# Narrower warm-up matmuls and another waiting point for early loads, in a fused attention and gated-MLP kernel

## The chip, the cores and the metric

The kernel runs on one core of a Trainium2 chip. The time is device microseconds for one launch. Matrix products run on TensorE (PE in the profile, its weight loads PEld), elementwise work on VectorE (DVE), ScalarE (ACT) and GpSimd (POOL). SyncE (SP) computes nothing; its queue, and ScalarE's and GpSimd's, issue the loads and stores.

## What is computed

With S = 2048 tokens of width D = 512, in bf16:

```python
x = A_x; xn = layernorm(x)
# A: attention of 32 heads of 16, each token sees 8 keys, 2 tokens apart
q, k, v = split(xn @ A_wqkv)
logits = einsum(q, k[pos - 2*w]) * Dh**-0.5          # w = 0..7, masked where pos - 2*w < 0
a = einsum(softmax(logits), v[pos - 2*w]) @ A_wo
# B: gated MLP that mixes over tokens
z = gelu(xn @ B_w_in)                                # 512 -> 1792
z1, z2 = z[..., :896], layernorm(z[..., 896:])
g = einsum('ts,sf->tf', B_w_sp, z2) + B_b_sp[:, None]
b = (z1 * g) @ B_w_out
return x + a + b
```

## The kernel before

The tokens lie in 16 blocks of 128, and the blocks in four groups of four. For each block, VectorE takes the statistics (`bnst`, line 612, and `bnag`, 615), GpSimd the power -0.5 (`rstd`, 617) and VectorE normalises (`norm`, 626). Blocks 0 to 3 are transposed on TensorE (`xTr`, 642) and copied out of PSUM by ScalarE (`xTe`, 648); later blocks go through transposing transfers on SP's queue (`xTd`, 630). Block 0 takes a short way: it is only centred (`ctr`, 621), in two halves, goes through TensorE so, and its scale is applied with the GELU; its normalised form follows later (`xNr`, 661, copied out at 665).

Then TensorE computes, in this order: the second half of z for blocks 0 to 3 (`z2`, 818, two matmul groups of 448 columns a block, GELU on ScalarE at 829), q and k of the first group (694, copied out at 702), v of blocks 0 to 7 (676), and so on group by group; then z1 (841), the token mixing g (951) and the output products (1017 and 1021).

Every operation is a task with the keys that it reads and writes. A planner (`Plan.schedule`) gives each engine its order, for the parts that matter from lists written out by hand (`plan.orders`), and `emit` places semaphore waits from the keys. A key that is read also protects it: whoever writes the same key later waits for all its readers. Engines and queues work in order.

The early loads, in the order of the queues:

- SP: x blocks 0 and 1; the first half (rows 0 to 255) of two 448-column pieces of `w_in` that make z2 (`w_in2a` and `w_in2b`); x blocks 3, 4, 5; q and k weights; x blocks 6 and 7; v weights; then x blocks 8 and on, whose eight buffers are those of blocks 0 and on (`ld_x`, line 545, slot `b % 8`), between the transposes of blocks 4 to 7.
- ScalarE: a priming activation (590), which loads the GELU table and reads a constant that GpSimd sets (524); then the second half (rows 256 to 511) of both z2 pieces (555), told to wait for VectorE's first memset, `zeros`; then x block 2.

The loads of q, k (567) and x blocks 4 to 7 are told to wait until x block 1 has landed, by naming it as read. That also makes them readers of block 1's buffer, which x block 9 uses next.

TensorE begins with a warm-up that has no use but to keep it busy: eight matmuls of 512 columns on a constant of ones (584). A shorter filler of 320 columns follows the transposes of block 0. Each matmul has a weight load of its own, of 128 columns.

Of the kernel before, what the change touches and what calls it, by code (L numbers as in the profile page):

```python
# [14 lines left out]
class Plan:  # L15
# [297 lines left out]
DEFAULT_CFG = dict(  # L313
    xdma=4,
    fill=1,
    warm=8,
    fill0=1,
    perm=0,
)
# [2 lines left out]
def build_kernel(nc, A_x, A_wqkv, A_wo, B_x, B_w_in, B_w_sp, B_b_sp, B_w_out, out, report=False, sched_kw=None,  # L322
                 cfg=None, emit=True):
    cfg = dict(DEFAULT_CFG, **(cfg or {}))
# [77 lines left out]
    with ExitStack() as es:  # L402
# [10 lines left out]
        def A(name, n, o2_=0):  # L413
            return ar[:, off[name] + o2_: off[name] + o2_ + n]

        def AC(o_, dims):
            return bass.AP(tensor=ar, offset=o_, ap=[[AR, 128]] + [list(d) for d in dims])
# [92 lines left out]
        def dma(eng, fn, nbytes, chan, reads=(), writes=(), name="", xbar=False, prio=None, lat=1700.0):  # L510
            return T(eng, fn, reads=tuple(reads), writes=tuple(writes), name=name, prio=prio,
                     dma=dict(chan=chan, nbytes=nbytes, xbar=xbar, lat=lat))

        ident = A("ident", 128)
        zeros = A("zeros", 512)
# [5 lines left out]
          name="steps0")  # L521
        T("dve", lambda v: v.memset(FCa(foff["st6"] + 8, [[9, NB], [1, 1]]), LN_EPS * D), writes=["st_eps"], est=160,
          name="steps1")
# [4 lines left out]
          writes=["ident"], est=350, name="ident1")  # L528
# [3 lines left out]
          writes=[("KTpad", c, 0) for c in range(4)], est=200, name="ktpad", prio=2)  # L532
# [7 lines left out]
        def xin_ap(sl):  # L540
            return A("xin", 512, 512 * sl) if sl < 4 else A("xin2", 512, 512 * (sl - 4))

        def ld_x(b, eng="sp", after=()):
            sl = b % 8
            dma(eng, lambda e: e.dma_start(xin_ap(sl), x2[128 * b:128 * b + 128, :]), 128 * 512 * 2,
                ("xin", sl), reads=after, writes=[("xin", sl)], name="ldx%d" % b)
# [6 lines left out]
        def ld_win_h(nm, lo, n):  # L553
            for h in range(2):
                dma(("sp", "act")[h], (lambda h: lambda e: e.dma_start(  # L555
                    AC(off["w_in"] + lo + 2 * 1792 * h, [[1792, 2], [1, n]]),
                    B_w_in[256 * h: 256 * h + 256, lo: lo + n].rearrange("(c p) n -> p c n", p=128)))(h),
                    256 * n * 2, (nm, h), reads=["zeros"] if h else [], writes=[(nm, h)], name="ld%s_%d" % (nm, h))

        ld_x(0)  # L560
        ld_x(1)
        ld_win_h("w_in2a", FH, HF)
        ld_win_h("w_in2b", FH + HF, HF)
        ld_x(2, "act")
        ld_x(3, "sp")
        for which, eng in ((0, "sp"), (1, "sp")):
            dma(eng, (lambda which: lambda e: e.dma_start(
                AC(off["wqk"] + 512 * which, [[1024, 4], [1, 512]]),
                A_wqkv[:, 512 * which: 512 * which + 512].rearrange("(c p) n -> p c n", p=128)))(which),
                512 * 512 * 2, ("wqk", which), reads=[("xin", 1)],  # L570
                writes=[(("wq", "wk")[which], c) for c in range(4)],
                name="ld%s" % ("qk"[which]))
        for b in range(4, min(8, NB)):
            ld_x(b, "sp", after=[("xin", 1)])
        dma("sp", lambda e: e.dma_start(A("wv_raw", 2048).rearrange("p (c n) -> p c n", c=4),
                                        A_wqkv[:, 1024:1536].rearrange("(c p) n -> p c n", p=128)),
            512 * 512 * 2, "wv", writes=["wv_raw"], name="ldwv")
# [2 lines left out]
        def filler(n, name, est, prio=None, reads=(), w=512):  # L580
            def warm(t):
                last = None
                for i in range(n):
                    last = t.matmul(ps[:, 3584: 3584 + w], ones[:, :128], ones[:, :w], start=True, stop=True)
                return last
            T("pe", warm, reads=reads, writes=[("ps", 7)], est=est, name=name, prio=prio)

        filler(cfg["warm"], "warm", 400.0 * cfg["warm"])

        T("act", lambda a: a.activation(Fv("prime", 4), mhalf, ACTF.Gelu_apprx_tanh), reads=["mhalf"], writes=["prime"],  # L590
          est=-1200, name="actprime", tbl="gelu")
# [545 lines left out]
def bass_parallel_sum__sliding_local_dilated__mixer_gmlp__prompt_kernel(  # L1137
    nc, A_x, A_wqkv, A_wo, B_x, B_w_in, B_w_sp, B_b_sp, B_w_out, out
):
    build_kernel(nc, A_x, A_wqkv, A_wo, B_x, B_w_in, B_w_sp, B_b_sp, B_w_out, out)  # L1140
# [28 lines left out]
```

## Time and profile before

| | |
|---|---|
| time, median of 3 runs | 237.5 us (235.75 to 238.12) |
| the profiled execution's own time | 236.43 us |
| its span, from the first to the last instruction | 234.6 us |
| TensorE busy | 230.8 us (98%) |
| VectorE busy | 202.4 us (86%) |
| ScalarE busy | 118.8 us (51%) |
| GpSimd busy | 51.1 us (22%) |
| moved by DMA | 41.76 MB, mean 178 GB/s |

The busy times are unions over one engine's instructions. A matmul's record reaches from its issue to the modelled end of its pass, so records overlap, and TensorE's busy share says that it always had something under way, not that it ran at its peak. In rows of the timeline the columns are the start in us from the span's start, the length, the engine, the line, the operation with its tiles, and how many were merged; in brackets stands how long the engine had been idle before it and what released it.

### The profile page before, as it was taken

Reading aid. Unit: us, or ns where it says so; the run is one execution under the profiler, and the core shown is the slowest. Engines: PE = TensorE matmul, PEld = TensorE weight load, DVE = VectorE, ACT = ScalarE, POOL = GpSimd, SP = SyncE. Lnnn points to the kernel's source line nnn. Section 1 sums busy time; section 2 is a strip of 40 time slices with the busy share of each in tenths; the row PEclk is TensorE's granted clock in tenths of the full one; section 3 lists DMA queues with packets and bytes.
Section 4 is the critical chain, followed back from the end, with each engine's and each line's share of the span. In section 5 each row is a group of like instructions: output and inputs, shape, how many; then the busy total and the mean of one; then the engine's idle time right before and its main releaser. Section 6 shows DMA issues by size and latency. Waiting matters only on the chain.

```text
span 234.6 us, 2976 instructions
## 1 busy us (share of the span) xinstructions
PE 230.8 (98%) x1107; PEld 110.5 (47%) x1107; DVE 202.4 (86%) x231; ACT 118.8 (51%) x235; POOL 51.1 (22%) x67
## 2 busy tenths in 40 slices
PE   8999999999999999999999999999999999999995
PEld 2554455454554444444444444444444444444444
DVE  4787979998989989997999994999999999999600
ACT  3798488988989978953021124232223413201442
POOL 4454973771690050001201000010000000000000
PEclk9999999999999999999999999999999999999999
DMA  6976770299909899691529999999545987802322
GB/s 210 357 188 145 176 163 0 92 191 322 375 33 179 198 245 264 119 237 41 155 64 220 287 228 225 297 231 307 157 134 157 203 237 187 227 0 46 92 63 70
DMA packets 87166, 41.76 MB, mean 178 GB/s; under 512 B 66272, under 2 KB 86000, under 8 KB 87152
## 3 DMA queue, kind: packets, MB, share of 16 engines
q1 hardware_dynamic: 71072, 23.24, 47.0%
q10 hardware_dynamic: 14640, 14.13, 20.1%
q0 software_dynamic: 1440, 4.21, 5.8%
q8 instruction: 9, 0.15, 0.3%
q14 instruction: 5, 0.04, 0.1%
HBM read 20.05 MB, written 5.26 MB: 108 GB/s over the span
## 4 chain that ended last, share of the span: by engine, by line
PE 95%; DMA 2%; DVE 1%; ACT 1%; POOL 0%; ACTq 0%; issue 0%
PE ps L951 41%; PE ps L694 12%; PE ps L1021 10%; PE ps L841 10%; PE ps L818 9%; PE ps L1017 6%; PE ps L676 6%; DMA arena<-in_A_x_dram 2%; ACT L590 0%; DVE fpool L612 0%; PE ps L642 0%; POOL fpool L617 0%; ACTq L555 0%; DVE arena L626 0%; ACT arena L1030 0%
## 5 line engine op out<-in xcount | busy, mean ns | idle before, releaser
L951 PE MATMUL ps<-arena 128*128 128x512 bf16 x448 | 97.5, 379 | 0.0
L951 PEld LDWEIGHTS ps<-arena 128*128 128x128 bf16 x448 | 43.8, 98 | 52.8
L945 ACT ACTIVATE ps<-arena 128x512 f32<-128x512 bf16 x28 | 16.5, 599 | 56.9 <-DVE arena L958 56.6
L718 DVE TENSOR_TENSOR arena<-arena 128x4096 bf16<-128x4096 bf16 x16 | 36.1, 2284 | 0.5 <-ACT arena L702 0.4
L976 DVE TENSOR_TENSOR arena<-arena 128x4096 bf16<-128x4096 bf16 x16 | 36.3, 2286 | 0.2
L980 DVE TENSOR_TENSOR arena<-arena 128x4096 bf16<-128x4096 bf16 (+1 forms) x16 | 28.1, 1755 | 0.3
L694 PE MATMUL ps<-arena 128*128 128x512 bf16 x128 | 28.3, 379 | 0.0
L723 DVE TENSOR_TENSOR arena<-arena 128x4096 bf16<-128x4096 bf16 x12 | 27.5, 2288 | 0.2
L1021 PE MATMUL ps<-arena 128*128 128x512 bf16 (+2 forms) x126 | 27.1, 355 | 0.0
L818 PE MATMUL ps<-arena 128*128 128x448 bf16 x128 | 26.2, 357 | 0.1
L841 PE MATMUL ps<-arena 128*128 128x512 bf16 x112 | 24.3, 379 | 0.0
L694 PEld LDWEIGHTS ps<-arena 128*128 128x128 bf16 x128 | 14.5, 113 | 13.2
L1030 ACT ACTIVATE arena<-ps 128x512 bf16<-128x512 f32 (+2 forms) x17 | 9.5, 559 | 21.4 <-PE ps L1021 20.5
L958 DVE TENSOR_TENSOR arena<-ps,arena 128x512 bf16<-128x512 f32 x28 | 19.1, 683 | 0.1
L1021 PEld LDWEIGHTS ps<-arena 128*128 128x128 bf16 x126 | 13.6, 113 | 11.0
L818 PEld LDWEIGHTS ps<-arena 128*128 128x128 bf16 x128 | 12.2, 98 | 11.7 <-issue 0.7
L846 ACT ACTIVATE arena<-ps 128x512 bf16<-128x512 f32 x28 | 15.9, 595 | 3.2 <-PE ps L841 2.7
L702 ACT ACTIVATE arena<-ps 128x1024 bf16<-128x1024 f32 x16 | 16.3, 1021 | 2.4 <-PE ps L694 1.6
L829 ACT ACTIVATE arena<-ps 128x448 bf16<-128x448 f32 x30 | 16.2, 546 | 2.2 <-issue 0.2
L841 PEld LDWEIGHTS ps<-arena 128*128 128x128 bf16 x112 | 11.0, 98 | 13.1
L708 POOL COPY arena<-arena 128x16 bf16<-128x16 bf16 x12 | 14.6, 1224 | 9.9 <-ACT arena L829 5.0
L1017 PE MATMUL ps<-arena 128*128 128x512 bf16 (+2 forms) x72 | 16.8, 355 | 0.0
(65 smaller groups left out, 193.5 us busy)
## 6 DMA issues: line engine op xcount, KB each, us to landing
arena<-vscr ACTq DMA_DIRECT2D x8, 1152.0 KB, 7.8
arena<-in_A_x_dram ACTq DMA_DIRECT2D x17, 128.0 KB, 5.0
vscr<-arena POOLq DMA_DIRECT2D x16, 128.0 KB, 2.5
arena<-in_A_x_dram SPq DMA_DIRECT2D x15, 128.0 KB, 3.9
out_dram<-arena ACTq DMA_DIRECT2D x15, 128.0 KB, 1.9
arena<-in_A_wqkv_dram SPq DMA_DIRECT2D x3, 512.0 KB, 6.2
ascr<-arena POOLq DMA_DIRECT2D x4, 256.0 KB, 4.0
arena<-ascr POOLq DMA_DIRECT2D x4, 256.0 KB, 3.3
```

Source lines behind the costliest of these rows:

```text
L694: last = t.matmul(bank(k + which), AC(off["wqk"] + 1024 * dc + col0, [[4, 128]]), AC(off["xnT"] + dc * S + 512 * j, [[1, 512]]), start=(dc ...
L718: T("dve", lambda v: v.tensor_tensor(pbv, qb, kb, ALU.mult), reads=[("QT", c, j), ("KT", c, j), ("KTpad", c, j)], writes=[("pb", s_)], est ...
L723: T("dve", lambda v: v.tensor_tensor(A("pb", 4096, 4096 * a), A("pb", 4096, 4096 * a), A("pb", 4096, 4096 * b), ALU.add), reads=[("pb", b) ...
L818: last = t.matmul(ps[:, 512 * k: 512 * k + HF], st, AC(off["w_in"] + 1792 * dc + c0, [[1, HF]]), start=(h == first and dc == 2 * h), stop= ...
L841: lastm = t.matmul(bank(k), AC(off["w_in"] + 1792 * dc + 128 * fc, [[1, 128]]), AC(off["xnT"] + dc * S + 512 * j, [[1, 512]]), start=(dc = ...
L945: T("act", lambda a: a.activation(bank(k), A("bbc", 512, 512 * tc), ACTF.Copy), reads=["bbc"], writes=[("ps", k)], est=c_act(512), name="g ...
L951: last = t.matmul(bank(k), AC(off["z2"] + FH * sh + 128 * fc, [[1, 128]]), AC(off["wT"] + WSL * r_ + sh * 512, [[1, 512]]), start=False, s ...
L958: T("dve", lambda v: v.tensor_tensor(uv, bank(k), uv, ALU.mult), reads=[("ps", k)], writes=[("z1T", fc, tc)], est=c_dve(512) + 20, name="u ...
L976: T("dve", (lambda iv, tv, av: lambda v: v.tensor_tensor(tv, iv, av, ALU.mult))(iv, tv, av), reads=[("attn", j), ("Ve", par)], writes=[("V ...
L980: T("dve", (lambda n: lambda v: v.tensor_tensor(AC(off["Vs"], [[4096, 2], [1, n]]), AC(off["Vs"], [[4096, 2], [1, n]]), AC(off["Vs"] + n, ...
L1017: t.matmul(po, AC(off["OT"] + 512 * ot_pos(tb) + 128 * cc, [[1, 128]]), AC(off["wo"] + 512 * cc + c0, [[1, n]]), start=False, stop=False, ...
L1021: last = t.matmul(po, AC(off["z1T"] + fc * S + t0, [[ts, 128]]), AC(off["w_out"] + 512 * fc + c0, [[1, n]]), start=False, stop=(fc == FC - ...
```

## The change

Three things change, and the hand-written orders stay as they are.

- The warm-up is 28 matmuls of 146 columns (4088 columns) where it was 8 of 512 (4096). The planner's estimate for it is nearly the same (3192 ns for 3200).
- The loads of q, k and x blocks 4 to 7 wait for the second half of `w_in2b`, which ScalarE's queue loads, where they waited for x block 1. They all stand on SP's queue behind x block 3.
- The second halves of the z2 weights on ScalarE's queue no longer wait for `zeros`.

As the wait no longer names x block 1, x block 9 no longer waits for the loads of q, k and blocks 4 to 7. In the order that the planner makes, it moves ahead of the four transposing transfers of blocks 4 to 7 on SP's queue. All other engines keep their order.

```diff
 DEFAULT_CFG = dict(
     xdma=4,
     fill=1,
-    warm=8,
+    warm=28,
...
-                    256 * n * 2, (nm, h), reads=["zeros"] if h else [], writes=[(nm, h)], name="ld%s_%d" % (nm, h))
+                    256 * n * 2, (nm, h), writes=[(nm, h)], name="ld%s_%d" % (nm, h))
...
-                512 * 512 * 2, ("wqk", which), reads=[("xin", 1)],
+                512 * 512 * 2, ("wqk", which), reads=[("w_in2b", 1)],
...
         for b in range(4, min(8, NB)):
-            ld_x(b, "sp", after=[("xin", 1)])
+            ld_x(b, "sp", after=[("w_in2b", 1)])
...
-        filler(cfg["warm"], "warm", 400.0 * cfg["warm"])
+        filler(cfg["warm"], "warm", 114.0 * cfg["warm"], w=146)
```

The filler that both use:

```python
def filler(n, name, est, prio=None, reads=(), w=512):
    def warm(t):
        for i in range(n):
            last = t.matmul(ps[:, 3584: 3584 + w], ones[:, :128], ones[:, :w], start=True, stop=True)
        return last
    T("pe", warm, reads=reads, writes=[("ps", 7)], est=est, name=name, prio=prio)
```

## The prediction

> **What bounds the kernel now.** I read the page's busy shares first, then the chain that ended last (in order of time: start, length, what), then who waited for whom on TensorE over the whole run.
>
> ```profile
> PE 230.8 (98%) x1107; PEld 110.5 (47%) x1107; DVE 202.4 (86%) x231; ACT 118.8 (51%) x235; POOL 51.1 (22%) x67
> ...
> 2.17 5.09 DMA arena<-in_A_x_dram
> ...
> 10.23 0.80 PE ps L818 x4
> 13.53 6.91 PE ps L694 x32
> 20.44 6.91 PE ps L676 x32
> ...
> PE ps L584 <- PEq L1154: 0.8, 1, 0.8
> PE ps L642 <- DVE arena L626: 0.3, 1, 0.3
> ```
>
> Only two waits stand for TensorE in the whole run, and the last ends at 9.35 us. From 10.23 us the chain is matmuls piece on piece to 232 us, so a change to the head is worth what it moves that stretch, and no more. Ahead of it the chain is one load: x block 2, issued third on ScalarE's queue (2.17 us), landed at 7.26, then its statistics, POOL's power and its normalisation. These are the rows of the head, from the timeline (start, length, what, idle before it and its releaser):
>
> ```profile
> 4.39 0.61 PE L642 MATMUL ps<-arena 128*128 128x128 bf16 x4
> ...
> 6.11 0.41 DVE L626 TENSOR_SCALAR arena<-arena,fpool 128x512 bf16<-128x512 bf16 x1 [0.46 <-POOL fpool L617]
> ...
> 6.98 0.39 PE L642 MATMUL ps<-arena 128*128 128x128 bf16 x4
> ...
> 7.29 0.69 DVE L612 BATCH_NORM_STATS2 fpool<-arena 128x6 f32<-128x512 bf16 x1 [0.77 <-DMA arena<-in_A_x_dram]
> ...
> 7.30 0.66 ACT L648 ACTIVATE arena<-ps 128x256 bf16<-128x256 f32 x2 [1.81 <-PE ps L642]
> ...
> 9.30 0.21 ACT L829 ACTIVATION_READ_ACCUMULATOR arena<-ps,fpool 128x1 f32 x1
> ...
> 9.34 0.23 PEld L642 LDWEIGHTS ps<-arena 128*128 128x128 bf16 x4 [0.74 <-DVE arena L626]
> ...
> 9.67 0.66 ACT L648 ACTIVATE arena<-ps 128x256 bf16<-128x256 f32 x2 [0.15 <-PE ps L642]
> ...
> 10.38 0.10 PEld L818 LDWEIGHTS ps<-arena 128*128 128x128 bf16 x1 [0.16 <-ACT arena L648]
> ```
>
> Three engines are close to one another here. VectorE waits 0.77 us for x block 2. TensorE's weight loads wait 0.74 us for that block's normalisation (9.34). But ScalarE, from 7.30 on, waits only 0.15 us (9.67) before block 2's evictions, and TensorE needs those at 10.38. That 0.15 us is what decides.
>
> **Part 1: x block 2 sooner.** These are ScalarE's second z2 load and x block 2 with their time from issue to landing, the DMA by stretch (the last number is GB/s), and two issues ahead of them:
>
> ```profile
> L555 ACTq DMA_DIRECT2D arena<-in_B_w_in_dram x1: 482/482/482, 1.7 to 1.7; - x1
> DMA to landing us min/median/max: 4.3/4.3/4.3
> L545 ACTq DMA_DIRECT2D arena<-in_A_x_dram x1: 488/488/488, 2.2 to 2.2; - x1
> DMA to landing us min/median/max: 5.1/5.1/5.1
> ...
> 1.50:3.00 1.50, 1.50 (x5) 0.59 (x4) 0.00 (x0) 0.72 (x2) 0.82 (x3) 1.00 0.68 131
> 3.00:7.26 4.26, 4.12 (x20) 1.45 (x18) 2.87 (x8) 0.66 (x2) 1.31 (x2) 1.00 1.08 367
> ...
> 0.73 0.10 POOL L524 MEMSET fpool<- 128x4 f32 x1 [0.29 <-POOLq L1154]
> 1.16 0.47 ACTq L555 DMA_DIRECT2D arena<-in_B_w_in_dram  x1
> ```
>
> 1.5 x 131 + 4.26 x 367 = 1760 KB had moved when x block 2 landed. The four x blocks and four z2 pieces that TensorE needs first are 1442 KB (by their shapes, 4 x 131 + 4 x 229); so some 300 KB of blocks 4, 5 and q went ahead of it. Held back, they free 300/367 = 0.8 us: landing near 6.45. Not holding ScalarE's z2 loads for the memset moves ScalarE's three issues from 1.16, 1.66 and 2.17 to at earliest about 0.9 (the prime activation still stands in front and waits for POOL's memset at 0.83): 0.2 to 0.3 us, on a DMA that moves only 131 GB/s up to 3.0. I take landing at 6.3 to 6.5. The bounds are 7.26 (the order on the wire is unchanged) and 6.2.
>
> Then the gain is cut down step by step. VectorE finishes block 1's normalisation at 6.52, so statistics of block 2 start at 6.55, not 7.29: 0.74 us. Block 2's transposes then are ready at about 8.6, but TensorE's earlier work ends at 9.34 - 0.74 = 8.60, or 0.1 later with the last matmul: 0.65 us remain. ScalarE, in order, is busy from 7.30 to 9.51 with work that hangs on block 1 and the z2 weights, so its eviction of block 2 starts at 9.52 in place of 9.67: **0.15 us** remain, and TensorE's 10.38 becomes 10.23. What could move ScalarE's 7.30 is block 1's transposes at 6.98; they stand in order behind z2 matmuls of block 0, which are not waiting for a load but run slowly:
>
> ```profile
> 6.05 0.15 PEld L818 LDWEIGHTS ps<-arena 128*128 128x128 bf16 x1
> 6.42 0.10 PEld L818 LDWEIGHTS ps<-arena 128*128 128x128 bf16 x1 [0.21 <-issue]
> 6.61 0.10 PEld L818 LDWEIGHTS ps<-arena 128*128 128x128 bf16 x1
> ```
>
> The pitch of 448-column matmuls is 0.37 us up to 6.42 and 0.19 us after it, though the clock column says 1.00 throughout. So the z2 weights' earlier landing (5.96, needed at 6.05) buys nothing. Term: -0.15 us, bounds 0 and -0.55 (the pitch falls one group sooner, block 1's transposes go at 6.6, right after the normalisation that ends at 6.52: 0.38 more).
>
> **Part 2: 28 narrow warm-ups.** 28 x 146 = 4088 columns for 4096. The wide ones go at one per 0.425 us:
>
> ```profile
> 2.00 0.15 PEld L584 LDWEIGHTS ps<-const-bfloat16-1.0 128*128 128x128 bf16 x1 [0.28 <-issue]
> 2.43 0.15 PEld L584 LDWEIGHTS ps<-const-bfloat16-1.0 128*128 128x128 bf16 x1 [0.28 <-issue]
> ...
> 4.69 0.31 PE L642 MATMUL ps<-arena 128*128 128x128 bf16 x1
> ```
>
> By columns, a narrow one takes 146/512 x 0.425 = 0.121 us, 28 of them 3.39 us against 3.40. What is added is 20 weight loads. The nearest row for a narrow matmul with a weight load of its own before the fast pitch is block 0's four transposes, at 4.39 to 4.69: three steps in 0.30 us, 0.10 each, half of that set by VectorE's second half. So a 0.12 us pitch hides the load: term 0. Bounds: nothing below (the columns are the same), and above as the rival on the other side.
>
> The Trainium skill ("TensorE: Matmul & The Clock Gate", Part 3, The mechanism) says that a weight load overlaps matmuls in flight only when its row group differs, and these fill all rows. By that rule the warm-up would take 28 x (0.12 + 0.15) = 7.5 us and the sum would be +2.9 us. The trace disagrees: four transposes, each with a load, fit into 0.61 us.
>
> **Part 3: the loads behind x block 3.** SP's queue waits at block 4 for ScalarE's second z2 load, in place of x block 1. Behind it stand blocks 4, 5, q, k, 6, 7, v, 8 and on. These are SP's issues of blocks 4 and 5, of q and k with their landing, and TensorE's first weight loads that follow q:
>
> ```profile
> L545 SPq DMA_DIRECT2D arena<-in_A_x_dram x2: 340/386/432, 3.8 to 4.2; - x2
> L567 SPq DMA_DIRECT2D arena<-in_A_wqkv_dram x2: 434/471/508, 4.6 to 5.1; - x2
> DMA to landing us min/median/max: 4.9/5.6/6.2
> ...
> 13.18 2.89 PEld L694 LDWEIGHTS ps<-arena 128*128 128x128 bf16 x14
> ```
>
> ScalarE's second z2 load landed at 1.66 + 4.3 = 5.96, and will a little earlier. So block 4 goes out at 5.5 to 6.0 in place of 3.8, q at 6.5 to 7.0 in place of 4.6, k half a us behind. The bytes ahead of k are the same; added is a pause on the wire from 6.4 (the first 1442 KB are through) to about 7.0 (I allow the new issue 1.3 us until its bytes move; the 131 GB/s up to 3.0 show such a start), 0.4 to 0.9 us. So k lands at 5.1 + 6.2 + 0.4 to 0.9 = 11.7 to 12.2, q at about 10.5 to 11. TensorE wants q at 13.18 and k 0.86 us later (32 matmuls take 6.91). Cost 0, hidden by z2 of blocks 2 and 3; if that cover goes, every us late costs a us. Upper bound, with both taking the longest time seen for a 512 KB piece, v's:
>
> ```profile
> L575 SPq DMA_DIRECT2D arena<-in_A_wqkv_dram x1: 434/434/434, 6.7 to 6.7; - x1
> DMA to landing us min/median/max: 6.9/6.9/6.9
> ...
> 20.36 0.69 DVE L612 BATCH_NORM_STATS2 fpool<-arena 128x6 f32<-128x512 bf16 x1 [1.58 <-DMA arena<-in_A_x_dram]
> ```
>
> q at 7.0 + 6.9 = 13.9 against 13.0: +0.9 us. v then lands near 15.9, wanted at 20.44. Blocks 6 and 7 land some 0.5 us late for VectorE, and TensorE wants their transposes only with V of these blocks, from 20.44 + 6 x 0.86 = 25.6 on: the cover is many times the delay.
>
> One load also moves: x block 9 reuses block 1's buffer. Before, the loads told to wait for block 1 counted as its readers, so block 9 stood behind four transposes; now it goes ahead of them. VectorE's 1.58 us wait at 20.36 should go. The chain has no VectorE there: 0 us, and the order of everything else is the same.
>
> **Sum.** -0.15 + 0 + 0 = -0.15 us against the profiled 236.43 us (span 234.6, 1.8 around it), which lies 1.1 us under the median 237.5. On the median's footing: 237.35, given as **237.3 us**. The runs shown spread by 2.4 us, so 1% is about what a measurement of this kernel can tell from no change; the forecast is "no difference".
>
> **The rivals.**
> - *Nothing moves at all*: the queues share the wire so that holding back blocks 4 and 5 doesn't bring block 2. For it: block 2 was issued ahead of blocks 4 and 5 (2.17 against 3.8) and may owe them nothing. Against it: the 300 KB. 237.5 us; 0.2.
> - *The warm-up is paced by its weight loads* (the other side). TensorE's warm-up ends at 4.18 and the first transposes wait for VectorE until 4.39, so it decides from a pitch of 3.62/28 = 0.129 us. If the 0.15 us loads set the pitch, 4.2 us: 0.5 us late; if nothing overlaps, 7.5 us, first transposes at 8.3, block 1's at about 9.9 in place of 6.98: +2.9, 240.4 us. Against it: the 0.10 us step. 0.07.
> - *q or k late*: +0.9 us, 238.3 us. For it: q is issued 2 us later and fewer than 2 us lie between landing and use. Against: the wire. 0.08.
> - *The fast pitch comes at another moment*: if not at 6.42 but a stretch as long as the warm-up (3.4 us) later, ten 448-column matmuls and six transposes cost 10 x 0.18 + 6 x 0.05 = 2.1 us more, less the 0.65 us idle: +1.5, 238.9 us; sooner: -0.55, 236.9 us. Nothing in the change asks for either. 0.05 each.
>
> **How the numbers follow.** Forecast 0.55, the rest as above. All but the unhidden weight loads stay within 1% of 237.5; I give that extreme 0.05, and two mishaps together or the runs' spread (the lowest shown is 0.7% under the median, the highest 0.3% over) 0.08: slower 0.13. Faster by over 1% would need 2.4 us out of a head whose TensorE waits are 0.8 + 0.3: only spread, 0.07. Same 0.80. The range goes from the lowest run shown less 0.35 (235.4) to the late clock with a little of the spread (239.4).
>
> **What would show it.** Right: SP's block 4 issued at 5.5 to 6.0; block 2's statistics at 6.55; the weight-load wait at 9.34 shrinks to about 0.1; ScalarE has no wait at block 2's evictions; q's first weight load within 0.3 us of 13.0 with no DMA wait; narrow matmuls at 0.12 us; VectorE's wait at 20.36 gone with no gain. Wrong: a TensorE wait on a wqkv load or on an eviction of Q/K after 13 us, a warm-up that ends after 4.4, or matmuls that turn fast much before or after 6.4.

## The result, and the profile after

| | before | after |
|---|---|---|
| median of 22 runs each, us | 236.38 (235.75 to 238.47) | 235.69 (235.36 to 236.09) |
| profiled execution, us | 236.43 | 235.56 |
| its span, us | 234.6 | 233.7 |

The ratio is 0.9953 [0.9937, 0.997]: the change makes the kernel faster by about half a per cent. The forecast said 237.3 us and no difference. Three things went into the miss, and the rest of the document separates them: the head became shorter by more than 0.15 us (by 0.2 to 0.25 us in the typical span); nearly half of the time saved lies outside the span, where the prediction had no term; and the footing of 237.5 us, a median of three runs, was itself 1.1 us too high. Executions at a reduced clock, or over 1.5% longer than a kernel's fastest, are left out of the ratios and of what is called undisturbed below; the profiled execution of the second run of after (span 303.9 us, granted clock 0.756) is one.

The first row is from the page of after, engine by engine.

```profile
PE 229.1 (98%) x1108; PEld 112.6 (48%) x1127; DVE 202.5 (87%) x231; ACT 119.2 (51%) x235; POOL 51.3 (22%) x67
```

Only PE and its weight loads moved: 20 weight loads more, as the change says. The 1.7 us less of matmul records can't be read as a gain, since after's trace lacks 19 matmul records that before's has (8 of them at line 951), though both kernels issue these matmuls. The chain that ended last (start, length, what) shows where the head went:

```profile
0.73 2.38 DMA arena<-in_A_x_dram
...
5.27 1.31 PE ps L818 x6
...
6.62 0.40 PE ps L642 x4
...
10.64 2.27 PE ps L818 x12
...
12.97 1.24 PE ps L694 x5
```

x block 2's load, 5.09 us of the chain before, is no longer on it. The chain now starts with x block 0 and reaches TensorE at 4.52; from 5.27 it is TensorE's own work almost piece on piece, with x block 2 in time. Before, q and k began on the chain at 13.53, now at 12.97. Behind that point little is changed: from q's first weight load to the end of the span lie 234.6 - 13.18 = 221.42 us before and 233.7 - 12.56 = 221.14 us after. These are the rows of the head of after, from the timeline (start, length, idle before it and its releaser in brackets):

```profile
0.74 3.30 PEld L584 LDWEIGHTS ps<-const-bfloat16-1.0 128*128 128x128 bf16 x28 [0.74 <-issue]
...
1.85 0.49 ACTq L545 DMA_DIRECT2D arena<-in_A_x_dram  x1
...
4.49 0.24 PEld L642 LDWEIGHTS ps<-arena 128*128 128x128 bf16 x4 [0.46 <-issue]
...
5.27 0.11 PEld L818 LDWEIGHTS ps<-arena 128*128 128x128 bf16 x2 [0.47 <-ACT arena L648]
...
5.53 0.61 PEld L818 LDWEIGHTS ps<-arena 128*128 128x128 bf16 x4
...
6.48 0.69 DVE L612 BATCH_NORM_STATS2 fpool<-arena 128x6 f32<-128x512 bf16 x1
...
6.62 0.40 PE L642 MATMUL ps<-arena 128*128 128x128 bf16 x4
...
6.94 0.66 ACT L648 ACTIVATE arena<-ps 128x256 bf16<-128x256 f32 x2 [1.45 <-PE ps L642]
...
8.59 0.24 PEld L642 LDWEIGHTS ps<-arena 128*128 128x128 bf16 x4 [0.34 <-ACT arena L829]
...
9.04 0.67 ACT L648 ACTIVATE arena<-ps 128x256 bf16<-128x256 f32 x2
...
9.76 0.22 PEld L818 LDWEIGHTS ps<-arena 128*128 128x128 bf16 x2 [0.16 <-ACT arena L648]
...
12.56 3.54 PEld L694 LDWEIGHTS ps<-arena 128*128 128x128 bf16 x17
```

Set against the rows of before: block 1's transposes go at 6.62 in place of 6.98, ScalarE takes them at 6.94 in place of 7.30, and everything on ScalarE behind them comes earlier, so block 2's evictions go at 9.04 in place of 9.67. That is the step the prediction had as fixed ("ScalarE, in order, is busy from 7.30"). What moved it is the pitch of TensorE's matmuls. Block 0's four transposes show it, by line (ns of one: shortest, middle, longest; then when they started), first before:

```profile
L642 PE MATMUL ps<-arena x4: 287/309/314, 4.4 to 4.7; 128*128 128x128 bf16 x4
```

and after:

```profile
L642 PE MATMUL ps<-arena x4: 216/218/225, 4.5 to 4.7; 128*128 128x128 bf16 x4
```

TensorE is already fast at 4.49 in after, where before it turned fast between 6.05 and 6.42. The weight loads agree: those of these transposes take 103 to 132 ns each before and 96 to 99 ns after, and the filler's behind them 0.15 and 0.10 us. The clock column says 1.00 in both kernels, so the pitch must be read from the rows.

### The profile page after: what moved, and what is told of

The parts are those of the page before. It is cut to its first block, busy times and chain, and to the rows that moved or that the text cites. A ratio compares the mean times of both kernels' runs of the same rounds, so it can differ in the third digit from the quotient of the medians.

```text
span 233.7 us, 2996 instructions
## 1 busy us (share of the span) xinstructions
PE 229.1 (98%) x1108; PEld 112.6 (48%) x1127; DVE 202.5 (87%) x231; ACT 119.2 (51%) x235; POOL 51.3 (22%) x67
## 4 chain that ended last, share of the span: by engine, by line
PE 96%; DMA 1%; issue 1%; DVE 1%; ACT 0%
PE ps L951 41%; PE ps L694 12%; PE ps L818 11%; PE ps L1021 10%; PE ps L841 10%; PE ps L1017 6%; PE ps L676 6%; DMA arena<-in_A_x_dram 1%; PE ps L642 1%; DVE fpool L612 0%; ACT arena L648 0%; DVE arena L621 0%; ACT arena L1030 0%; PE ps L661 0%; DVE fpool L615 0%
## 5 line engine op out<-in xcount | busy, mean ns | idle before, releaser
L818 PE MATMUL ps<-arena 128*128 128x448 bf16 x128 | 25.7, 353 | 0.2 <-ACT arena L648 0.2
L851 ACT ACTIVATE arena<-arena 128x896 bf16<-128x896 bf16 x16 | 15.1, 943 | 0.1
```

Of the source, the lines that this page charges most:

```text
L818: last = t.matmul(ps[:, 512 * k: 512 * k + HF], st, AC(off["w_in"] + 1792 * dc + c0, [[1, HF]]), start=(h == first and dc == 2 * h), stop= ...
```

## The experiments

The theories were these. *Pitch*: the narrow warm-up itself makes TensorE fast sooner, and that pulls block 1's transposes, and ScalarE with them, forward. *Loads*: the gain is x block 2's earlier landing, by the wait or by the un-held z2 weights. *Block 9*: the load that moved takes away stalls much later in the run. *Chance*: the kernels differ by which executions were drawn.

This table puts the heads side by side. Each line is one profiled execution, so it shows mechanisms and not effects; the medians of spans are over all undisturbed runs of the kernel (that of before is of the 34 beside the two halves; it is the same beside after again, and 234.1 beside the row that waits for block 1), and the ratio is of times to the kernel before on the same chip.

| kernel | z2 weights waited for by PE's loads, us | block 2's statistics at | q's first weight load at | its span | median span | ratio |
|---|---|---|---|---|---|---|
| before | 0.5 | 7.29 | 13.18 | 234.6 | 234.15 | |
| before, again | 1.0 | 6.98 | 13.01 | 234.2 | 234.2 | 1.0006 [0.9982, 1.0031] |
| narrow warm-up alone | 1.3 | 7.26 | 13.20 | 234.3 | 234.05 | 0.9982 [0.9965, 0.9998] |
| loads alone | 0.9 | 6.85 | 13.00 | 234.2 | 233.95 | 0.9984 [0.9962, 1.0006] |
| after, z2 held as before | 1.0 | 7.13 | 13.02 | 234.2 | 234.0 | 0.9977 [0.9961, 0.9993] |
| after, waiting for block 1 as before | 0.7 | 6.23 | 12.54 | 233.7 | 233.9 | 0.9981 [0.9961, 1.0002] |
| after | 0 | 6.48 | 12.56 | 233.7 | 233.9 | 0.9953 [0.9937, 0.997] |

### Each half by itself

The narrow warm-up alone, on the kernel before:

```diff
-    warm=8,
+    warm=28,
-        filler(cfg["warm"], "warm", 400.0 * cfg["warm"])
+        filler(cfg["warm"], "warm", 114.0 * cfg["warm"], w=146)
```

> The kernel before, with the 28 warm-up matmuls of 146 columns and nothing else. Theory A (the narrow warm-up brings the fast matmul pitch forward, from about 6.4 us to about 4.2 us, and the early x block 2 then lets the head use it): block 0's transposes at 4.4 us already show a weight load of 0.10 us instead of 0.13 to 0.15, block 1's transposes go at 6.6 instead of 6.98, but block 2 still lands near 7.2, so the first q weight load stays within 0.15 us of 13.18 and the time is 0 to 0.2 us under before; the upper tail of before's times (237.5 to 238.5 in 7 of 22) is gone. Theory B (the moment of the fast pitch is chance from run to run, and the loads bring all of the gain): fast pitch near 6.4 again, time as before, with the same upper tail.

Measured: 235.99 us (12 runs), ratio 0.9982 [0.9965, 0.9998]. Its row of the transposes, by line:

```profile
L642 PE MATMUL ps<-arena x4: 219/224/231, 4.2 to 4.5; 128*128 128x128 bf16 x4
```

So the fast pitch comes with the narrow warm-up and needs nothing of the loads. But in the timeline the gained time runs into the loads:

```profile
6.08 0.49 PEld L818 LDWEIGHTS ps<-arena 128*128 128x128 bf16 x4 [0.91 <-DMA arena<-in_B_w_in_dram]
...
7.26 0.69 DVE L612 BATCH_NORM_STATS2 fpool<-arena 128x6 f32<-128x512 bf16 x1 [0.92 <-DMA arena<-in_A_x_dram]
...
7.47 0.11 PEld L818 LDWEIGHTS ps<-arena 128*128 128x128 bf16 x2 [0.41 <-DMA arena<-in_B_w_in_dram]
```

The faster TensorE now waits for the z2 weights, twice, and x block 2 comes as late as before. In this execution q starts at 13.20: nothing was won at q.

The loads alone, on the kernel after:

```diff
-    warm=28,
+    warm=8,
-        filler(cfg["warm"], "warm", 114.0 * cfg["warm"], w=146)
+        filler(cfg["warm"], "warm", 400.0 * cfg["warm"])
```

> The changed kernel with the wide warm-up of before (8 x 512). Theory A: the fast pitch comes near 6.4 us as before, block 1's transposes go near 7.0, ScalarE sets the pace, the first q weight load moves by 0.15 us only (13.0), the time is 0.1 to 0.2 us under before and the upper tail of the times stays. Theory B: q's first weight load near 12.6 and 0.6 to 0.7 us under before, like the whole change.

Measured: 235.93 us, 0.9984 [0.9962, 1.0006], no difference that can be told. By line and in the timeline:

```profile
L642 PE MATMUL ps<-arena x4: 265/311/311, 4.4 to 4.6; 128*128 128x128 bf16 x4
```

```profile
6.60 0.11 PEld L818 LDWEIGHTS ps<-arena 128*128 128x128 bf16 x2 [0.54 <-DMA arena<-in_B_w_in_dram]
...
6.85 0.69 DVE L612 BATCH_NORM_STATS2 fpool<-arena 128x6 f32<-128x512 bf16 x1 [0.45 <-DMA arena<-in_A_x_dram]
...
9.48 0.66 ACT L648 ACTIVATE arena<-ps 128x256 bf16<-128x256 f32 x2
```

The pitch is the slow one again, block 2 is 0.44 us sooner than before, and ScalarE takes its evictions at 9.48, right behind its other work: 0.19 us sooner. This is what the prediction's Part 1 worked out (9.52), on the kernel that has only that part.

The kernel before once more:

> The kernel before, once more, to see another execution of it. Theory A: the fast pitch near 6.4 us again or later (9 to 10 us in one of the slow executions that make the upper tail), ratio 1.000. Theory B: the fast pitch anywhere from 4 to 10 us, ratio 1.000.

Measured: 236.61 us, ratio 1.0006 [0.9982, 1.0031], span 234.2 in the profile, q at 13.01, transposes slow (287 to 314 ns). So 0.17 us at q and 0.4 us of span lie between two executions of one kernel, and the pair of profiles at the head of this section overstates the change: by the medians of spans the narrow warm-up is worth 0.1 us, the loads 0.2 and both 0.25. In single executions each half meets the other's bound; the medians, with steps of 0.1 us in a span, can't tell whether the halves simply add up. The table's first column warns of the same: the landing of the z2 weights varies by about a us between executions (0 to 1.3 us of wait with un-held weights, over all kernels here), so after's missing wait is partly luck.

The kernel after was run again too.

> The changed kernel again, beside the kernels with one part alone. Theory A (both parts are needed, as either leaves the other limit standing): transposes of block 0 with 0.10 us weight loads, first q weight load at 12.5 to 12.7, 0.5 to 0.7 us under before, more than narrow alone (0.2) and loads alone (0.3) together or about their sum. Theory B (what the parts bring adds up, and the head of 12.56 was one lucky execution): q at 12.6 to 13.1, 0.3 us under before at most.

Measured: 235.76 us beside 236.19 for before, 0.9969 [0.9951, 0.9986] (12 runs). Of its profile only the head is used here: its transposes at 4.4 us were fast (216 to 227 ns). The gain repeats, somewhat smaller, with intervals that overlap.

### The wait, or the weights that are not held

After with the z2 weights held for `zeros` again:

```diff
-    256 * n * 2, (nm, h), writes=[(nm, h)], name="ld%s_%d" % (nm, h))
+    256 * n * 2, (nm, h), reads=["zeros"] if h else [], writes=[(nm, h)], name="ld%s_%d" % (nm, h))
```

> The changed kernel, but ScalarE's z2 loads wait for the memset again, as before. Theory A with the wait point as the part that counts: x block 2 lands 0.2 to 0.3 us later than in the changed kernel (6.2 to 6.3, not 5.9), which is still before VectorE is free for it at 6.5, so q's first weight load stays at 12.5 to 12.7 and the time within 0.1 us of the changed kernel. Rival (the hold is what counts): block 2 lands near 7.2, q near 13.0 or later, 0.4 us slower than the changed kernel.

Measured: 235.8 us, 0.9977 [0.9961, 0.9993]. In the timeline:

```profile
6.12 0.49 PEld L818 LDWEIGHTS ps<-arena 128*128 128x128 bf16 x4 [0.95 <-DMA arena<-in_B_w_in_dram]
...
7.13 0.69 DVE L612 BATCH_NORM_STATS2 fpool<-arena 128x6 f32<-128x512 bf16 x1 [0.77 <-DMA arena<-in_A_x_dram]
```

After with blocks 4 to 7, q and k waiting for block 1 again:

```diff
-                512 * 512 * 2, ("wqk", which), reads=[("w_in2b", 1)],
+                512 * 512 * 2, ("wqk", which), reads=[("xin", 1)],
-            ld_x(b, "sp", after=[("w_in2b", 1)])
+            ld_x(b, "sp", after=[("xin", 1)])
```

> The changed kernel, but with the loads behind block 3 waiting for x block 1 as before (so x block 9 is behind the transposes too); narrow warm-up and no hold on ScalarE's z2 loads. Theory A: x block 2 lands 0.3 us earlier than before (6.9), its statistics start near 6.95, q's first weight load at 12.8 to 13.0, the time between narrow alone and the whole change (0.3 us under before). Theory C adds: the few long runs of before (span 0.6 us or more over the others) are still there, as block 9 is late again.

Measured: 235.87 us, 0.9981 [0.9961, 1.0002]. In the timeline:

```profile
5.59 0.49 PEld L818 LDWEIGHTS ps<-arena 128*128 128x128 bf16 x4 [0.47 <-DMA arena<-in_B_w_in_dram]
...
6.23 0.68 DVE L612 BATCH_NORM_STATS2 fpool<-arena 128x6 f32<-128x512 bf16 x1
...
12.54 1.17 PEld L694 LDWEIGHTS ps<-arena 128*128 128x128 bf16 x6
```

The answer is the opposite of what the prediction said. With the new wait but held weights, VectorE waits 0.77 us for block 2, as it did in before (0.77). With the old wait but un-held weights it doesn't wait for it at all. The fifteen profiles of all kernels here say the same: x block 2 landed between 6.95 and 7.3 us in the five with held weights (mean 7.1, and 7.1 with the new wait) and between 5.9 and 7.0 us in the ten without (mean 6.4, and 6.1 with the old wait). ScalarE's three issues, 0.3 us sooner, bring x block 2 by 0 to 1.3 us; an effect of holding back blocks 4, 5 and q is not seen, though each of the two crossed cases has one profile only. Of the time, the runs can't rank the two: 235.8 and 235.87 us, beside 235.76 for after on the chip of the first.

### How narrow is narrow

The same columns in all, in other pieces: 10 of 409, 14 of 292 (twice) and 32 of 128, each on the kernel after.

```diff
-    warm=28,                 filler(..., 114.0 * cfg["warm"], w=146)
+    warm=10,                 filler(..., 319.0 * cfg["warm"], w=409)
+    warm=14,                 filler(..., 228.0 * cfg["warm"], w=292)
+    warm=32,                 filler(..., 100.0 * cfg["warm"], w=128)
```

> The changed kernel with 10 warm-up matmuls of 409 columns (4090). If any narrower matmul than 512 turns the pitch: transposes of block 0 with 0.10 us weight loads, q at 12.5 to 12.7. If it takes more weight loads in the same time (14 were enough, 8 were not): transposes still at 0.13 us, fast pitch near 6.3, q near 13.0 and the time as with the loads alone, 235.9 us.

> The changed kernel with 14 warm-up matmuls of 292 columns, 4088 columns in all, between the two sizes. Theory A, if what counts is the share of time in which weights are loaded beside matmuls: in between, the fast pitch comes either at 4.2 us or at 6.4 us, and the time is that of the whole change (235.7 us) or of the loads alone. Theory A, if what counts is any narrower matmul: as the whole change. Theory B: the size doesn't matter, 235.7 us.

> The changed kernel with 14 warm-up matmuls of 292 columns, once more. If its long executions (6 of 11 with a span of 234.7 or more, in the profile a wait of 1.2 us for the attention output's transpose near 171 us) belong to this size: again near half of them long, median near 237. If they were that session's: median 235.7 and at most one long, as with 28 or 32.

> The changed kernel with 32 warm-up matmuls of 128 columns (4096 in all), the narrowest for which a weight load can still hide behind a matmul. Theory A: transposes of block 0 with 0.10 us weight loads, q at 12.5 to 12.7, time as the changed kernel within 0.1 us. Rival from the prediction (the weight loads set the pace): pitch over 0.12 us, warm-up ends 0.1 to 0.9 us later, q later by as much.

Measured, with the shortest and longest record of block 0's transposes in each profile:

| warm-up | profiles: transposes, ns | matmuls fast from, us | median us | ratio |
|---|---|---|---|---|
| 8 x 512 | four: 265 to 314, all slow | 5.15; about 6.0; by 6.31; 6.42 | | |
| 10 x 409 | 266 to 314, slow | 6.19 | 236.04 | 0.9982 [0.9964, 1.0] |
| 14 x 292 | 216 to 226, fast | by 4.72 | 237.1 | 1.001 [0.9981, 1.0039] |
| 14 x 292, again | 266 to 314, slow | 5.37 | 236.39 | 1.0008 [0.9985, 1.0031] |
| 28 x 146 | seven: six fast (216 to 231), one slow (264 to 314) | six by 4.5, the other 4.97 | 235.69 (after) | 0.9953 [0.9937, 0.997] |
| 32 x 128 | 219 to 284, the last fast | 4.49 | 235.64 | 0.9966 [0.9944, 0.9987] |

The four of 8 x 512 are, by the moment, the early block 9 below, the loads alone, before again and before. So the wide warm-up has no fixed moment either. In the timeline, the first two 448-column matmuls of z2 in before again and in the early block 9:

```profile
5.24 0.90 PE L818 MATMUL ps<-arena 128*128 128x448 bf16 x2
```

```profile
5.15 0.54 PE L818 MATMUL ps<-arena 128*128 128x448 bf16 x2
```

In the second, the 320-column filler at 4.59 had still been slow (0.47 us, for 0.30 at the fast pitch). So with one warm-up the moment varies by about 1 us between executions, and chance has a share. But chance alone would seldom give this table: of the eleven profiles with 8 or 28 pieces five have slow transposes, and four profiles picked blindly would all be among these five in 5 of 330 ways. The moment depends on the pieces, then, and in between it is a toss: 14 x 292 came out once each way. 32 x 128 is level with after (235.64 and 235.69 us), 10 x 409 between it and before. The Trainium skill ("TensorE: Matmul & The Clock Gate", Part 1, What's actually happening) says that the warm-up is a span of time of about 3.4 us and not a number of matmuls. The trace agrees for 28 x 146, whose loads run from 0.74 to 4.04; time alone doesn't give the moment for 8 x 512, which is as long and without a gap, and is followed by slow matmuls for 0.5 to 2 us more. Whether the number of matmuls counts, the share of weight loads, or the short gaps between pieces, these runs don't tell.

Taken together, the profiles show that q needs both halves. In the five with un-held weights and transposes that end fast, q's first weight load stands at 12.34 to 12.89 us (after, the old wait, 14 x 292, 32 x 128, and the order put back below); in the other nine at 12.88 to 13.28, among them the early block 9, fast from 5.15 but with held weights (12.94), and 10 x 409, with un-held weights but slow (12.88). The second run of after is left out.

The 14 x 292 kernels also lose time that has nothing to do with the head. In the timeline of the first, SP's queue and TensorE:

```profile
145.26 14.70 SPq L880 DMA_TRANSPOSE arena<-in_B_w_sp_dram  x1
...
171.88 1.04 PE L1017 MATMUL ps<-arena 128*128 128x512 bf16 x4 [1.18 <-DMA arena<-arena]
```

and of the second:

```profile
173.69 1.04 PE L1017 MATMUL ps<-arena 128*128 128x512 bf16 x4 [2.47 <-DMA arena<-arena]
```

A transposing transfer of `w_sp` holds SP's queue for 14.70 us, and for 13.44 in the second (the longest of the four in before is 9.29, in after 12.90), the transpose of the attention's output (989) is issued behind it, and TensorE waits for that. The spans of 234.7 us and more, 15 of before's 115 undisturbed runs beside the experiments and none of after's 33, are 9 of 20 for 14 x 292. Why this kernel meets the stall more often isn't shown.

### x block 9

First block 9's load was put back behind block 7's transposing transfer, and more than wished: this edit waits for the *landing* of that transfer, not only for its issue.

```diff
-                    ld_x(b)
+                    ld_x(b, after=[("xnT", 7)] if b == 9 else ())
```

> The changed kernel, with x block 9 loaded behind the four transposes again, as in the order of before. If TensorE is the only bound: VectorE waits about 1.6 us at block 9's statistics again, and the time is that of the changed kernel within 0.1 us. Rival (VectorE's freed time shows at the end, by earlier transposes of the attention output): 0.2 to 0.3 us slower, or single executions with a wait of TensorE at about 170 us.

Measured: 238.46 us, 1.0091 [1.0058, 1.0125] (8 runs), the only kernel that is clearly slower. Its timeline and its waits (engine, tile and line, waited for: us in all, times, longest):

```profile
23.95 0.69 DVE L612 BATCH_NORM_STATS2 fpool<-arena 128x6 f32<-128x512 bf16 x1 [4.19 <-DMA arena<-in_A_x_dram]
...
32.45 2.10 PE L694 MATMUL ps<-arena 128*128 128x512 bf16 x8 [0.70 <-ACT arena L680]
```

```profile
PE ps L951 <- ACT ps L945: 1.4, 1, 1.4
PE ps L694 <- ACT arena L680: 1.1, 2, 0.7
```

VectorE's wait at block 9 grew from 1.58 to 4.19 us, and TensorE, which the prediction saw decoupled from VectorE there, stalled 1.1 us on v's evictions at 32 us and 1.4 us later. The slack that hid 1.58 us is used up somewhere below 4.19.

Then only the order was put back:

```diff
+        plan.orders.append("xTd7 ldx9".split())
```

> The changed kernel with x block 9 behind the four transposes on SP's queue by order alone, without the wait for the last transpose's landing that the earlier try had by mistake. Theory C (block 9's place counts: its statistics hold up GpSimd's power for it, the stores of v behind that on GpSimd's queue, ScalarE's evictions of v and so TensorE at 30 to 33 us; the earlier try was so late, 4.2 us of VectorE's wait, that it lost 2.3 us, and before stands 1.6 us into the same wait): VectorE waits 1 to 2.5 us at block 9, ScalarE waits 3 us or more on the stores of v in all, the time is 0.1 to 0.6 us over the changed kernel and a few of the runs are 1 us or more over it. Theory A alone (TensorE's head is all): as the changed kernel within 0.1 us, no such runs.

Measured: 235.58 us, 0.9978 [0.9956, 1.0001] (12 runs).

```profile
19.88 0.69 DVE L612 BATCH_NORM_STATS2 fpool<-arena 128x6 f32<-128x512 bf16 x1 [1.43 <-DMA arena<-in_A_x_dram]
```

The wait is back and the median is no worse than after's, against the 0.1 to 0.6 us that theory C expected; two of its 11 undisturbed runs are long (spans of 234.8 and 235.8), as it did expect. And the early block 9 alone, on the kernel before, with a key of its own for block 1's landing:

```diff
-                ("xin", sl), reads=after, writes=[("xin", sl)], name="ldx%d" % b)
+                ("xin", sl), reads=after, writes=[("xin", sl)] + (["x1in"] if b == 1 else []), name="ldx%d" % b)
...
-            ld_x(b, "sp", after=[("xin", 1)])
+            ld_x(b, "sp", after=["x1in"])
```

> The kernel before, with x block 9 ahead of the four transposes and nothing else: the loads still wait for x block 1, but no longer count as readers of its buffer. Theory C (block 9's place makes the long executions): typical span as before (234.1), none of 12 with a span of 234.7 or more where before has about one in six, median time 0.1 to 0.3 us under before. Theory A alone: as before in median and in long executions.

Measured: 236.49 us, 1.0009 [0.9989, 1.0029].

```profile
18.46 0.69 DVE L612 BATCH_NORM_STATS2 fpool<-arena 128x6 f32<-128x512 bf16 x1
```

The wait is gone and nothing is won. For the typical time the theory of block 9 falls both ways round; as predicted, the move is worth 0 there. What it may do to the rare long spans stays open. With block 9 late and the narrow warm-up they are 4 of 34 (narrow alone 0 of 12, order put back 2 of 11, old wait 2 of 11). With it early they are 0 of 57 (after, z2 held and 32 x 128), 0 of 24 with the wide warm-up (loads alone, and block 9 alone) and 1 of 12 for 10 x 409, but 9 of 20 for 14 x 292, which has it early too. The last experiment can't decide it: the 22 runs of before beside it had none either.

### What lies outside the span

Part of the gain is in no trace. Over undisturbed runs, mean time is mean span plus what lies around it: for before 236.40 = 234.26 + 2.14 (115 runs beside the experiments), for after 235.70 = 233.88 + 1.82 (33). So of 0.70 us, 0.38 is span and 0.32 is around it. Without the 15 long spans before's mean is 234.12, so the 0.38 is made of 0.23 for the typical span, which the head can explain, and 0.15 for the long ones. Only a third of the gain is explained, then. The time around the span is typically 1.8 us; it exceeds 2.1 us in 64 of 150 runs with the 8 x 512 warm-up (before, loads alone, early block 9 alone) and in 5 of 99 with 28 or 32 narrow pieces. The kernels with one half only don't tell on which half it hangs (4 of 12 for the loads alone, 3 of 12 for the narrow warm-up alone). Nor does it simply follow the pitch: 10 x 409, slow in its profile, has 1 of 12. In all four groups of before's runs it is frequent (10 to 12 of 22 to 34), so it isn't one chip's or one hour's. With the narrow warm-up and either part of the loads it is 0 or 1 of 11 or 12. What this time is, and why it mostly goes along with the warm-up, stays open. With it goes the spread of the runs: 0.73 us between the lowest and the highest of after, 2.72 for before.

## Why the prediction was wrong, point by point

- **The rival "the fast pitch comes at another moment" is what happened.** It had 0.05 for "sooner", with the sentence "Nothing in the change asks for either". That is the step that failed: the narrow warm-up moves the pitch (the narrow warm-up alone, and six of seven profiles with 28 pieces). The 6.42 us that the prediction took as given came from one execution; three others with the wide warm-up were fast between 5.15 and 6.31. The rival's price was about right: -0.55 us forecast in that case, 13.18 to 12.56 = -0.62 for q in the pair of profiles, though only 0.2 to 0.25 less in the medians of spans. Part 2 costed the warm-up by how long it takes, which was right (0.121 us a matmul; its 28 loads end at 4.04), and gave it the term 0, which left out what it does to the matmuls behind it. That every narrow matmul's weight load would be hidden was right; the extreme of 7.5 us was not seen (the loads take 3.30 in all).
- **Part 1's split was the wrong way round.** It gave 0.8 us of x block 2's earlier landing to holding back blocks 4, 5 and q, and 0.2 to 0.3 us to the un-held z2 weights. In the profiles the un-held weights bring it with the old wait too (6.23, no wait), and the new wait without them doesn't (7.13, 0.77 us of wait). Dividing bytes by a rate, as if the 300 KB stood in one line ahead of block 2, was the faulty step. The landing itself, 1.85 + 4.1 = 5.95 us, was sooner than the forecast 6.3 to 6.5.

By line, ScalarE's load of x block 2 in after:

```profile
L545 ACTq DMA_DIRECT2D arena<-in_A_x_dram x1: 488/488/488, 1.8 to 1.8; - x1
DMA to landing us min/median/max: 4.1/4.1/4.1
```

- **How Part 1 cut the gain down was right, and so was its 0.15 us for the loads by themselves.** In the loads alone ScalarE's evictions of block 2 moved by 0.19 us, and the time by less than the runs can tell. The same cut-down named 7.30 on ScalarE as the thing that would have to move; it moved to 6.94 by the pitch.
- **"The z2 weights' earlier landing buys nothing"** held at the slow pitch only. With the fast pitch and the weights held, the weight loads wait 1.0 and 1.3 us for them (z2 held; narrow alone), up from 0.5 and 1.0 at the slow pitch; in after's profile they don't wait.
- **Part 3 was right where it mattered.** Block 4 was issued at 5.5, q at 6.4 and k at 6.8; they landed 4.8 and 5.8 us later, at 11.2 and 12.66 (forecast 10.5 to 11 and 11.7 to 12.2), before TensorE's use at 12.56 and 0.86 later. The margin of k is 0.8 us. Too small was "some 0.5 us late" for block 6: it landed at 13.03 in place of 11.69, 1.3 us late, and its statistics waited 1.82 us, hidden all the same. VectorE's wait at 20.36 went, with no gain, as said.

In after, SP's issues of q and k with their landing, by line, and block 6's statistics in the timeline:

```profile
L567 SPq DMA_DIRECT2D arena<-in_A_wqkv_dram x2: 434/471/508, 6.4 to 6.8; - x2
DMA to landing us min/median/max: 4.8/5.3/5.8
```

```profile
13.05 0.69 DVE L612 BATCH_NORM_STATS2 fpool<-arena 128x6 f32<-128x512 bf16 x1 [1.82 <-DMA arena<-in_A_x_dram]
```

- **The footing.** "On the median's footing" put the forecast 1.1 us above the profiled execution because the median of three runs did. With 22 runs before's median is 236.38, at the profiled 236.43. Of the 1.6 us between 237.3 and 235.69, this step makes 1.1. The range held the time only because it reached down to the lowest of the three runs.
- **No term for what lies outside the span.** The sum took "1.8 around it" as fixed; before has 2.14 on average and after 1.82. By size this is the larger miss: the forecast change was -0.15 us and the means differ by -0.70, of which -0.23 is the typical span, -0.32 the time around it and -0.15 the rare long spans. For the last two the prediction had no term, and their cause stays open.

## What to carry to other kernels

A warm-up is to be judged by the pitch of the matmuls behind it, read from their rows and weight loads, and not by its length or the clock column; the same columns in more and smaller pieces made it work sooner here. Where a pitch, a load and another engine end within half a us of one another, each part of a change alone runs into the next bound within one profiled execution, so cost the parts together, and read the effect from many runs, since one pair of profiles here showed 0.9 us of span where the medians show 0.2 to 0.25. Three runs with a spread of 1% are no footing: put the forecast where the profiled execution and the lower runs agree.

## What the runs showed of the hardware that was not expected

- After eight matmuls of 512 columns from 0.74 to 4.2 us TensorE is fast from 5.15 to 6.42 us on, with slow transposes in four profiles of four; after 28 of 146 columns over the same time it is fast by 4.5 us in six of seven and from 4.97 in the other.
- 0.3 us at the issue of ScalarE's loads moved x block 2's landing by 0.7 us on average and by up to 1.3 us (7.26 to 5.95), while holding back 128 KB and 512 KB transfers on SP's queue left it where it was (7.1 with held weights).
- The time around the span isn't constant: over 2.1 us in 64 of 150 runs with the wide warm-up and in 5 of 99 with 28 or 32 pieces.
- The longest transposing transfer of `w_sp` holds SP's queue for 9.29 to 14.70 us between executions of nearly the same program; with 2.47 us of wait on TensorE behind it, it can cost more than this whole change brings.
